# A written order in place of a greedy share: merging channel mixing with attention and token mixing

## The chip, the cores and the metric

The kernel runs on one core of a Trainium2 chip. The metric is device time in microseconds for one execution; the median of the runs is given, and one further execution was taken with the hardware profiler. Engines: TensorE (PE in the profile; its weight loads are PEld), VectorE (DVE), ScalarE (ACT), GpSimd (POOL) and SyncE (SP).

## The reference

Windowed attention with sink columns (window 128, 4 sinks) on q, k, v of shape (4, 8, 768, 64), and a mixer block on its result x of shape (4, 768, 512):

```
scores = q @ k.T / 8, kept where key < 4 or 0 <= row - key < 128
x = softmax(scores) @ v, heads side by side                       # (4, 768, 512)
h = relu(x.T @ w_tok1) @ w_tok2                                   # token mixing: 768 -> 256 -> 768
u = x + h.T
out = u + relu(u @ w_ch1) @ w_ch2                                 # channel mixing: 512 -> 1536 -> 512
```

## The kernel before

**Work.** A "pair" is two heads of one batch: 16 pairs, four a batch. Attention of a pair: q and k are transposed on TensorE; scores are made keys by rows, as 128-key blocks of which each serves two 128-row blocks; ScalarE takes the exponential out of PSUM into `pT`, VectorE masks it; the sums with `v_aug` (a column of ones appended) go back to PSUM (`ps_o`), and VectorE takes the reciprocal of the ones' column (`recip`) and multiplies into `x_sb`. Token mixing works on half a batch's columns (`g` = 0 for pairs 0 and 1 of the batch, 1 for pairs 2 and 3): `mix_h` (x times `w_tok1`, then relu into `h1T`), three `mix_u` (times `w_tok2`, plus x, into `u_sb`), and `turned_u`, which transposes `u_sb`; the copies out of PSUM make `uT`. Channel mixing of a batch is 24 units `v1` (four matmuls of 384 columns, relu into `v1T`) and then 24 units `out_part` (three matmuls of 512 columns; after every fourth VectorE adds u into `o_sb` and SP stores it). The last row block of batch 3 is split into three units by columns instead. A burst is a unit that works with parts of the array (64 rows) instead of all 128: transposes, scores, sink scores and sink values of neighbouring pairs are put together in bursts.

**Queues of units.** The kernel is written as an instruction stream by a small planner in the kernel file (class `Plan`). Every TensorE unit is an `Op` with its estimated ns, what it depends on, what PSUM banks it needs and which operations follow it on the other engines. There are two tags of PSUM: `sc`, two large banks for scores and transposes, and `mx`, four banks for everything else; a bank is free when its readers are done. `run` gets three sorts of units: `first` (attention of pairs 0 to 3 and batch 0's token mixing, several lists), `main` (channel mixing of batches 0 to 3: 48 + 48 + 48 + 47 units, of which the first 24 of a batch are `v1`) and `side` (attention of pairs 4 to 15 and token mixing of batches 1 to 3: 75 units). The planner keeps a clock for each engine and appends the next instruction; the other engines' operations come in the order in which the planner lets them begin, `urgent` deciding between those that can begin at the same time on the same engine. The chip then runs each engine's instructions in the order so written and waits for semaphores.

**How side and main were merged.** `target(m)` says how much of the side work (in estimated ns) should be placed when `m` of the main work is: batch b's channel mixing carries the side work for batch b + 1 in its first 60%. If side is behind, the next side unit is taken if it can begin within 40 ns of the next main unit, otherwise main first; if one of the two cannot begin, the other is taken.

**The side units by number** (index in `side`, as written by `attention_and_tokens`). "A" is a pair's first burst: transposes of the next pair, the first scores of this pair, and the sink values of the pair before, whose two `mx` banks it takes. "V" are the two value units of the pair before, one a head. "B" is the pair's second burst: its other scores, sink scores for two pairs and, at some pairs, a `turned_u`.

```
 0, 1        transposes of pair 4: q, k
 2, 3        pair 4: A, B
 4, 5 6, 7   pair 5: A, V of 4, B
 8, 9 10, 11 pair 6: A, V of 5, B;       12, 13-15  mix_h, mix_u of batch 1, g = 0
16, 17 18,19 pair 7: A, V of 6, B
20, 21 22    pair 8: A, V of 7;  23, 24-26  mix_h, mix_u of batch 1, g = 1;  27  B (turned_u)
28, 29 30,31 pair 9: A, V of 8, B
32, 33 34,35 pair 10: A, V of 9, B;      36, 37-39  mix_h, mix_u of batch 2, g = 0
40, 41 42,43 pair 11: A, V of 10, B
44, 45 46    pair 12: A, V of 11;  47, 48-50  mix_h, mix_u of batch 2, g = 1;  51  B (turned_u)
52, 53 54,55 pair 13: A, V of 12, B
56, 57 58,59 pair 14: A, V of 13, B;     60, 61-63  mix_h, mix_u of batch 3, g = 0
64, 65 66,67 pair 15: A, V of 14, B
68 69        values of pair 15;  70, 71-73  mix_h, mix_u of batch 3, g = 1;  74  turned_u
```

**Lines of the profile.** Matmuls are L113, with tiles `ps_mx<-uT,w_ch` for `v1` and `ps_mx<-w_ch,v1T` for `out_part`; transposes are L441 (`turned_u`), L471 and L453; copies are L120 (ScalarE) and L122 (VectorE, GpSimd), relu L126 and L128; exponentials L555 and L594, masks L563; `recip` L663 and `x_sb` L666; `u_sb` L767; `o_sb` L940; L489 is the memset that clears the score bank after a pair's transposes were copied out of it (`cleared`). `kTs` are the sink columns of k, copied out of the same bank as `kT`.

Of the kernel before, what the change touches and what calls it, by code (L numbers as in the profile page):

```python
# [16 lines left out]
def kernel(  # L17
# [14 lines left out]
    B, H, S, D = q.shape  # L32
# [10 lines left out]
    D1 = D + 1  # L43
    scale = 1.0 / float(D) ** 0.5

    NQ = 6
    MASKED_BY_PE = [(p, g) for p in range(NHP) for g in range(NT // 2) if (p, g) != (NHP - 1, 0)]

    singles = ctx.enter_context(tc.tile_pool(name="singles", bufs=1))
    qkv_pool = ctx.enter_context(tc.tile_pool(name="qkv", bufs=NQ))  # L50
    raw_pool = ctx.enter_context(tc.tile_pool(name="raw", bufs=4))
# [60 lines left out]
    def mm(*args, **kwargs):  # L112
        in_order(nc.tensor.matmul(*args, skip_group_check=True, **kwargs))  # L113
# [19 lines left out]
    done = {}  # L133
# [55 lines left out]
    for n in range(4):  # L189
        i, odd = n // 2, n % 2  # L190
# [27 lines left out]
    SWITCH = 95.0  # L218
# [23 lines left out]
    class Plan:  # L242
# [60 lines left out]
        def commit_pe(self, op, t):  # L303
# [7 lines left out]
            op.done = self.free["PE"] + PE_OUT + SEM  # L311
            self.pending.extend(op.then)

        def run(self, first, main, side, target):

            first, main, side = [list(u) for u in first], list(main), list(side)
            m = s = 0.0
            while any(first) or main or side or self.pending:
                o = self.other()
                tm = self.start_pe(main[0]) if main else None  # L320
                ts = self.start_pe(side[0]) if side else None
                early = [(t, u) for u in first if u for t in [self.start_pe(u[0])] if t is not None]
                if early:
                    soonest = min(t for t in [tm, ts, *(t for t, _ in early)] if t is not None)
                    stay = [(t, u) for t, u in early if self.half and u[0].half and t <= soonest + SWITCH]
                    t, u = next((e for e in stay + early if e[0] <= soonest + (SWITCH if e in stay else 40.0)), (None, None))
                    if u is not None and (o is None or o[0] > t):
                        self.commit_pe(u.pop(0), t)
                        continue
                pick = None  # L330
                if tm is not None and ts is not None:
                    behind = s < target(m)
                    if behind:
                        pick = "side" if ts <= tm + 40.0 else "main"
                    else:
                        pick = "main" if tm <= ts + 40.0 else "side"
                elif tm is not None:
                    pick = "main"
                elif ts is not None:
                    pick = "side"  # L340
                t = {"main": tm, "side": ts, None: None}[pick]
# [10 lines left out]
                assert pick, "no unit can begin"  # L352
                if pick == "main":
                    op = main.pop(0)
                    m += op.size
                else:
                    op = side.pop(0)
                    s += op.size
                self.commit_pe(op, t)

    def unit(ns, fn, deps=(), need=None, then=(), half=False):

# [281 lines left out]
    def sink_values(p):  # L644

        b, hp = pairs[p]
        vsk = v_sinks[p % NHP]

        def run():
            for i in range(2):  # L650
                tiles["ps_o", p, i] = bank("mx", NT, D1)
            for qt in range(2, NT):
                for i in range(2):
                    rows = ds(D * i, D)
                    mm(
                        tiles["ps_o", p, i][:, qt], tiles["pT_sink", p][rows, ts(qt - 2, P)], vsk[rows, i],
                        start=(qt == 2), stop=False,
                    )

        for i in range(2):  # L660
            def recip(e, i=i):
                r = tiles["recip", p, i] = pt_pool.tile([P, NT, 1], FP32, name="recip")
                in_order(nc.vector.reciprocal(r, tiles["ps_o", p, i][:, :, D:D1]))  # L663

            def norm(e, i=i):
                in_order(nc.vector.tensor_tensor(  # L666
                    out=x_sb[b][:, :, ds((2 * hp + i) * D, D)], in0=tiles["ps_o", p, i][:, :, 0:D],
                    in1=tiles["recip", p, i].to_broadcast([P, NT, D]), op=ALU.mult,
                ))

            done["r", p, i] = Op({"DVE": 180.0}, recip)
            done["x", p, i] = Op({"DVE": 550.0}, norm, [done["r", p, i]])
            done["r", p, i].urgent = done["x", p, i].urgent = 1
        return piece(
            120, run, [done["p", p, NT], done["vs", p]], {"mx": [[done[n, p, i] for n in "rx"] for i in range(2)]}, [],
        )
# [185 lines left out]
    def attention_and_tokens():  # L862
# [5 lines left out]
        for p in range(first, last + 1):  # L868
# [6 lines left out]
            if p > first:  # L875
                pieces.append(sink_values(p - 1))
# [135 lines left out]
    plan = Plan()  # L1012
# [53 lines left out]
    plan.pending.append(done["masks"])  # L1066

    first = first_attention()
    main, side, sizes = [], [], []
    parts = attention_and_tokens()  # L1070
    for b in range(B):
        units = parts[b] if b + 1 < B else []
        channels = mix_channels(b)
        sizes.append((sum(u.size for u in channels), sum(u.size for u in units)))
        main += channels
        side += units

    def target(m):
        total = 0.0
        for n, (msize, ssize) in enumerate(sizes):  # L1080
            f = m / msize / 0.6
            if f < 1.0 or n == B - 1:
                return total + max(0.0, min(1.0, f)) * ssize if m < msize else total + ssize
            if m < msize:
                return total + ssize
            total += ssize
            m -= msize
        return total

    plan.run(first, main, side, target)  # L1090


# [33 lines left out]
```

## Time and profile before

| | |
|---|---|
| median of 3 runs | 208.69 us (208.69 to 209.34) |
| the profiled execution | 208.97 us, of which the span is 207.2 us |
| granted TensorE clock | 1.00 of full speed |
| TensorE | 200.0 us busy, 97% of the span, 2377 matmuls |
| VectorE | 113.0 us, 55%, 253 instructions |
| ScalarE | 116.8 us, 56%, 213 instructions |
| GpSimd | 67.4 us, 33%, 86 instructions |
| loads by GpSimd's queue, share of 16 DMA engines | 72.3% |

The span runs from the first to the last profiled instruction; the execution's own time has some 1.8 us around it. The timeline rows read: start, length (us), engine, line, operation, tiles out<-in, shapes, count of merged instructions, and in brackets the engine's idle time just before and what ended it. Matmul rows overlap: one matmul's record is longer than the distance to the next.

### The profile page before, as it was taken

Reading aid. Unit: us, or ns where it says so; the run is one execution under the profiler, and the core shown is the slowest. Engines: PE = TensorE matmul, PEld = TensorE weight load, DVE = VectorE, ACT = ScalarE, POOL = GpSimd, SP = SyncE. Lnnn points to the kernel's source line nnn. Section 1 sums busy time; section 2 is a strip of 40 time slices with the busy share of each in tenths; the row PEclk is TensorE's granted clock in tenths of the full one; section 3 lists DMA queues with packets and bytes.
Section 4 is the critical chain, followed back from the end, with each engine's and each line's share of the span. In section 5 each row is a group of like instructions: output and inputs, shape, how many; then the busy total and the mean of one; then the engine's idle time right before and its main releaser. Section 6 shows DMA issues by size and latency. Waiting matters only on the chain.

```text
span 207.2 us, 5542 instructions
## 1 busy us (share of the span) xinstructions
PE 200.0 (97%) x2377; PEld 119.9 (58%) x2377; DVE 113.0 (55%) x253; ACT 116.8 (56%) x213; POOL 67.4 (33%) x86
## 2 busy tenths in 40 slices
PE   6899999999999999999999999999999999999994
PEld 2455885566665565656656555666756545665443
DVE  4686654747678657866586562856663621000222
ACT  4699767869717446979494141979671103774000
POOL 6399759795599982540000000000000000000000
PEclk9999999999999999999999999999999999999999
DMA  6999999999999999595000212100001122000223
GB/s 208 289 247 185 174 173 191 153 155 192 160 168 153 205 189 202 53 90 38 3 0 5 101 54 101 55 0 3 0 3 51 54 101 101 0 3 0 101 101 101
DMA packets 73223, 21.58 MB, mean 104 GB/s; under 512 B 63216, under 2 KB 70256, under 8 KB 73200
## 3 DMA queue, kind: packets, MB, share of 16 engines
q0 software_dynamic: 67232, 11.80, 72.3%
q1 hardware_dynamic: 5968, 9.45, 12.8%
q8 instruction: 18, 0.29, 0.6%
q14 instruction: 5, 0.04, 0.1%
HBM read 26.75 MB, written 6.29 MB: 159 GB/s over the span
## 4 chain that ended last, share of the span: by engine, by line
PE 88%; DVE 5%; ACT 3%; DMA 2%; issue 1%; SPq 0%
PE ps_mx L113 75%; PE ps_sc L113 7%; DMA k_f<-in_k_dram 2%; PE ps_sc L471 2%; DVE kT L122 2%; ACT qT L120 1%; PE ps_mx L441 1%; PE ps_mx L453 1%; DVE x_sb L666 1%; ACT pT L555 1%; ACT v1T L126 1%; PE ps_mx L116 1%; DVE uT L122 0%; DVE recip L663 0%; DVE u_sb L767 0%
## 5 line engine op out<-in xcount | busy, mean ns | idle before, releaser
L113 PE MATMUL ps_mx<-uT,w_ch 128*128 128x384 bf16 x384 | 67.9, 326 | 1.3 <-DVE x_sb L666 1.0
L113 PE MATMUL ps_mx<-w_ch,v1T 128*128 128x512 bf16 (+2 forms) x312 | 65.3, 363 | 0.0
L126 ACT ACTIVATE v1T<-ps_mx 128x384 bf16<-128x384 f32 x85 | 41.0, 494 | 26.8 <-PE ps_mx L113 17.6
L113 PEld LDWEIGHTS <-w_ch 128*128 128x128 bf16 x384 | 35.6, 98 | 25.7 <-DVE x_sb L666 2.5
L555 ACT ACTIVATE pT<-ps_sc 128x1024 bf16<-128x1024 f32 (+1 forms) x48 | 44.8, 957 | 9.3 <-PE ps_sc L113 8.7
L113 PEld LDWEIGHTS <-v1T 128*128 128x128 bf16 x312 | 29.1, 98 | 29.5 <-issue 0.2
L940 DVE TENSOR_TENSOR o_sb<-ps_mx,u_sb 128x512 f32<-128x512 f32 x23 | 15.9, 690 | 41.9 <-PE ps_mx L113 41.7
L98 POOL DMA_DIRECT2D q_bf<-in_q_dram x24 | 19.7, 824 | 4.5 <-DMA w_ch<-in_moe_w_ch_dram 2.2
L98 POOL DMA_DIRECT2D k_bf<-in_k_dram x24 | 19.6, 822 | 4.6 <-DMA w_ch<-in_moe_w_ch_dram 3.1
L113 PEld LDWEIGHTS <-w_tok 128*128 128x128 bf16 x192 | 18.3, 98 | 4.7 <-issue 0.7
L122 DVE COPY kT<-ps_sc 128x768 bf16<-128x768 bf16 x11 | 10.5, 958 | 16.7 <-ACT qT L120 16.7
L106 POOL DMA_DIRECT2D v_aug<-in_v_dram x16 | 16.5, 1030 | 9.5 <-ACT v1T L126 6.1
L563 DVE TENSOR_TENSOR pT<-pT,mask_main 128x1024 bf16<-128x1024 bf16 (+1 forms) x24 | 14.6, 620 | 4.4 <-ACT pT L555 4.4
L767 DVE TENSOR_TENSOR u_sb<-ps_mx,x_sb 128x512 bf16<-128x512 f32 x20 | 12.7, 685 | 5.0 <-PE ps_mx L113 5.0
L113 PE MATMUL ps_sc<-qT,kT 64*64 64x192 bf16 (+3 forms) x288 | 15.2, 252 | 0.2 <-DVE ps_sc L489 0.2
L113 PE MATMUL ps_mx<-v_aug,pT 128*128 128x65 bf16 x352 | 15.2, 194 | 0.0
L113 PEld LDWEIGHTS <-pT 128*128 128x128 bf16 x352 | 13.4, 98 | 1.9 <-issue 0.6
L120 ACT ACTIVATE qT<-ps_sc 128x768 bf16<-128x768 bf16 x11 | 8.9, 812 | 7.6 <-PE ps_sc L471 7.5
L113 PE MATMUL ps_mx<-h1T,w_tok 128*128 128x256 bf16 x96 | 12.5, 273 | 0.0
L113 PE MATMUL ps_mx<-x_sb,w_tok 128*128 128x256 bf16 x96 | 12.0, 273 | 0.0
L666 DVE TENSOR_TENSOR x_sb<-ps_mx,recip 128x384 bf16<-128x384 f32 x22 | 11.9, 542 | 0.0
L113 PEld LDWEIGHTS <-kT 64*64 64x64 bf16 (+1 forms) x288 | 7.1, 103 | 6.7 <-issue 5.0
(74 smaller groups left out, 156.0 us busy)
## 6 DMA issues: line engine op xcount, KB each, us to landing
out_dram<-o_sb SPq DMA_DIRECT2D x23, 256.0 KB, 2.0
v_aug<-in_v_dram POOLq DMA_DIRECT2D x16, 192.0 KB, 7.2
w_ch<-in_moe_w_ch_dram POOLq DMA_DIRECT2D x8, 384.0 KB, 9.0
q_bf<-in_q_dram POOLq DMA_DIRECT2D x24, 96.0 KB, 7.1
k_bf<-in_k_dram POOLq DMA_DIRECT2D x24, 96.0 KB, 6.0
q_f<-in_q_dram SPq DMA_DIRECT2D x4, 384.0 KB, 5.4
k_f<-in_k_dram SPq DMA_DIRECT2D x4, 384.0 KB, 5.9
w_tok<-in_moe_w_tok_dram POOLq DMA_DIRECT2D x2, 384.0 KB, 8.5
```

Of the source, the lines that this page charges most:

```text
L98: in_order(nc.gpsimd.dma_start(out=out[:, h], in_=rows[:, h]))
L106: in_order(nc.gpsimd.dma_start(out=v_aug.rearrange("p i t d -> p (i t) d")[:, :, 0:D], in_=v[b].rearrange("h s d -> (h s) d")[2 * hp * S:2 ...
L113: in_order(nc.tensor.matmul(*args, skip_group_check=True, **kwargs))
L120: in_order(nc.scalar.activation(out, in_, AF.Copy))
L122: in_order({"DVE": nc.vector, "POOL": nc.gpsimd}[e].tensor_copy(out=out, in_=in_))
L126: in_order(nc.scalar.activation(out, in_, AF.Relu))
L471: in_order(nc.tensor.transpose(ps[:, x, n, j], bfs[p, n][rows, j], ident[rows, rows]))
L555: in_order(nc.scalar.activation(part(tiles["pT", p][:, :, ds(2 * g, 2)]), of_keys(tiles["ps_s", p, g])[:, :, 0:width(g)], AF.Exp, scale=scale,
L563: in_order(nc.vector.tensor_tensor(out=pt, in0=pt, in1=m, op=ALU.mult))
L666: in_order(nc.vector.tensor_tensor(out=x_sb[b][:, :, ds((2 * hp + i) * D, D)], in0=tiles["ps_o", p, i][:, :, 0:D], in1=tiles["recip", p, i ...
L767: in_order(nc.vector.tensor_tensor(out=u_part(b, g, s0, n), in0=tiles["ps_u", b, g, s0], in1=x_sb[b][:, s0:s0 + n, c0:c0 + cn], op=ALU.add,))
L940: in_order(nc.vector.tensor_tensor(out=o_sb.rearrange("p (g c) -> p g c", g=2), in1=u_rows(b, st), in0=tiles["ps_out", b, st].rearrange("p ...
```

## The change

The shares (`target` and the sizes) are gone. `MERGED` lists the 75 side units in the order in which they are to be placed, each with the number of main units that must be placed before it ("23/41": side unit 23 when 41 main units are placed). `run` takes a side unit as soon as its number is reached, and otherwise main, and waits on its clock for that unit even if one of the other sort could begin. Units of `first` may still go before the picked one. Besides, the `recip` and `x_sb` operations of pairs 4 to 14 get the urgency 3 in place of 1 (the memset of the score bank has 2, the relu of `v1` has 1).

```diff
+    MERGED = (
+        "1/0 0/2 2/4 3/8 4/15 5/15 6/17 7/19 8/23 9/24 10/24 12/27 11/27 13/29 15/30 14/31 16/32 17/33 18/33 "
+        "19/36 20/39 21/39 22/39 23/41 25/42 24/42 26/42 27/44 28/49 29/50 30/51 31/52 32/57 33/58 34/58 "
+        "36/61 35/62 38/62 37/64 39/67 40/67 41/69 42/69 43/73 44/78 45/78 46/79 47/83 49/85 48/85 50/85 "
+        "51/90 52/98 53/100 55/102 54/107 56/107 57/108 58/108 59/113 60/115 62/118 63/121 61/121 64/124 "
+        "65/126 67/128 66/128 68/133 69/133 70/137 73/139 72/139 71/139 74/142"
+    )
...
-        def run(self, first, main, side, target):
...
+        def run(self, first, main, side):
+
+            first, main = [list(u) for u in first], list(main)
+            order = [[int(n) for n in unit.split("/")] for unit in MERGED.split()]
+            side, behind = [side[n] for n, _ in order], [n for _, n in order]
+            placed = 0
             while any(first) or main or side or self.pending:
                 o = self.other()
                 tm = self.start_pe(main[0]) if main else None
                 ts = self.start_pe(side[0]) if side else None
+                pick = "side" if side and (not main or behind[0] <= placed) else "main"
+                t = tm if pick == "main" else ts
                 early = [(t, u) for u in first if u for t in [self.start_pe(u[0])] if t is not None]
...
-                pick = None
-                if tm is not None and ts is not None:
-                    behind = s < target(m)
-                    if behind:
-                        pick = "side" if ts <= tm + 40.0 else "main"
-                    else:
-                        pick = "main" if tm <= ts + 40.0 else "side"
-                elif tm is not None:
-                    pick = "main"
-                elif ts is not None:
-                    pick = "side"
...
                 if pick == "main":
-                    op = main.pop(0)
-                    m += op.size
+                    placed += 1
                 else:
-                    op = side.pop(0)
-                    s += op.size
-                self.commit_pe(op, t)
+                    behind.pop(0)
+                self.commit_pe((main if pick == "main" else side).pop(0), t)
...
-            done["r", p, i].urgent = done["x", p, i].urgent = 1
+            done["r", p, i].urgent = done["x", p, i].urgent = 3
```

More of the change, by code (lines that the diff above doesn't have):

```diff
@@ L312, in commit_pe @@
             self.pending.extend(op.then)
-        def run(self, first, main, side, target):
-            first, main, side = [list(u) for u in first], list(main), list(side)
-            m = s = 0.0
+        def run(self, first, main, side):
[3 more added lines that the diff above has]
+            placed = 0
             while any(first) or main or side or self.pending:
@@ L321, in run @@
                 ts = self.start_pe(side[0]) if side else None
+                pick = "side" if side and (not main or behind[0] <= placed) else "main"
+                t = tm if pick == "main" else ts
                 early = [(t, u) for u in first if u for t in [self.start_pe(u[0])] if t is not None]
                 if early:
-                    soonest = min(t for t in [tm, ts, *(t for t, _ in early)] if t is not None)
+                    soonest = min([t for t, _ in early] + ([] if t is None else [t]))
                     stay = [(t, u) for t, u in early if self.half and u[0].half and t <= soonest + SWITCH]
-                    t, u = next((e for e in stay + early if e[0] <= soonest + (SWITCH if e in stay else 40.0)), (None, None))
-                    if u is not None and (o is None or o[0] > t):
-                        self.commit_pe(u.pop(0), t)
+                    te, u = next((e for e in stay + early if e[0] <= soonest + (SWITCH if e in stay else 40.0)), (None, None))
+                    if u is not None and (o is None or o[0] > te):
+                        self.commit_pe(u.pop(0), te)
                         continue
-                pick = None
-                if tm is not None and ts is not None:
-                    behind = s < target(m)
-                    if behind:
-                        pick = "side" if ts <= tm + 40.0 else "main"
-                    else:
-                        pick = "main" if tm <= ts + 40.0 else "side"
-                elif tm is not None:
-                    pick = "main"
-                elif ts is not None:
-                    pick = "side"
-                t = {"main": tm, "side": ts, None: None}[pick]
                 if o is not None and (t is None or o[0] <= t):
@@ L351, in run @@
                     continue
-                assert pick, "no unit can begin"
+                assert t is not None, "no unit can begin"
                 if pick == "main":
-                    op = main.pop(0)
-                    m += op.size
-                else:
-                    op = side.pop(0)
-                    s += op.size
-                self.commit_pe(op, t)
+                    placed += 1
+                else:
+                    behind.pop(0)
+                self.commit_pe((main if pick == "main" else side).pop(0), t)
     def unit(ns, fn, deps=(), need=None, then=(), half=False):
@@ L1068 @@
     first = first_attention()
-    main, side, sizes = [], [], []
+    main, side = [], []
     parts = attention_and_tokens()
     for b in range(B):
[L1072 to L1090, printed above, removed]
+        main += mix_channels(b)
+        side += parts[b] if b + 1 < B else []
+    plan.run(first, main, side)
 _INS = ['q', 'k', 'v', 'n_sink', 'window', 'moe_w_tok1', 'moe_w_tok2', 'moe_w_ch1', 'moe_w_ch2']
```

## The prediction

> **What bounds the kernel now.** I began with the page: the span, the busy time of each engine and the chain that ended last.
>
> ```profile
> span 207.2 us, 5542 instructions
> PE 200.0 (97%) x2377; PEld 119.9 (58%) x2377; DVE 113.0 (55%) x253; ACT 116.8 (56%) x213; POOL 67.4 (33%) x86
> ...
> PE 88%; DVE 5%; ACT 3%; DMA 2%; issue 1%; SPq 0%
> ...
> L113 PE MATMUL ps_mx<-uT,w_ch 128*128 128x384 bf16 x384 | 67.9, 326 | 1.3 <-DVE x_sb L666 1.0
> ```
>
> TensorE is busy for 200.0 of 207.2 us and is 88% of the chain. The change alters no matmul, so it can only win or lose time in which TensorE waits. The windows of the stretch in which the list acts, from the first channel matmul near 30 us to the last side unit near 165, and of the rest after it, show how much there is.
>
> ```profile
> 29.80:148.00 118.20, 116.50 (x1569) 71.04 (x1568) 77.52 (x163) 75.72 (x143) 45.70 (x54) 1.00 1.04 101
> 148.00:165.00 17.00, 17.00 (x229) 10.71 (x229) 9.65 (x21) 6.92 (x12) 0.00 (x0) 1.00 0.09 32
> 165.00:207.20 42.20, 39.26 (x230) 21.31 (x228) 7.42 (x13) 12.19 (x25) 0.00 (x0) 1.00 0.17 63
> ```
>
> The columns are length, then busy time (and count) of PE, PEld, DVE, ACT and POOL, then the clock. Idle are 118.20 - 116.50 = 1.70 us before 148 us, nothing from there to 165, and at the end only the tail after the last matmul, which the list does not touch. The granted clock is 1.00 throughout. Who ends the idle time stands in the view of waits (engine, line, releaser: total, times, longest):
>
> ```profile
> PE ps_mx L113 <- DVE x_sb L666: 1.0, 4, 0.2
> ...
> PE ps_mx L113 <- DVE uT L122: 0.4, 1, 0.4
> ...
> PE ps_sc L113 <- DVE ps_sc L489: 0.2, 1, 0.2
> ```
>
> These are idle times after the modelled end of the matmul before (326 ns after its start, while matmuls follow each other more closely), so each true loss is larger. The timelines of TensorE, VectorE and ScalarE around the first wait on `x_sb` show it.
>
> ```profile
> 44.05 0.84 PE L113 MATMUL ps_mx<-v_aug,pT 128*128 128x65 bf16 x22
> 44.73 1.46 PE L113 MATMUL ps_mx<-uT,w_ch 128*128 128x384 bf16 x8
> 46.43 0.82 PE L113 MATMUL ps_mx<-uT,w_ch 128*128 128x384 bf16 x4 [0.23 <-DVE x_sb L666]
> 47.18 0.49 PE L113 MATMUL ps_sc<-qT,kT 64*64 64x192 bf16 x16
> 47.60 3.42 PE L113 MATMUL ps_mx<-uT,w_ch 128*128 128x384 bf16 x20
> ```
> ```profile
> 44.72 0.96 DVE L122 COPY kT<-ps_sc 128x768 bf16<-128x768 bf16 x1 [2.11 <-ACT qT L120]
> 45.59 0.26 DVE L663 RECIPROCAL recip<-ps_mx 128x6 f32<-128x6 f32 x2
> 45.81 0.56 DVE L666 TENSOR_TENSOR x_sb<-ps_mx,recip 128x384 bf16<-128x384 f32 x1
> ```
> ```profile
> 43.88 0.81 ACT L120 ACTIVATE qT<-ps_sc 128x768 bf16<-128x768 bf16 x1
> 45.71 0.35 ACT L120 ACTIVATE kTs<-ps_sc 64x4 bf16<-64x4 bf16 x2 [1.02 <-DVE kT L122]
> 46.09 1.02 ACT L555 ACTIVATE pT<-ps_sc 128x1024 bf16<-128x1024 f32 x1
> 47.01 1.25 ACT L126 ACTIVATE v1T<-ps_mx 128x384 bf16<-128x384 f32 x3
> ```
>
> The row of 20 gives the pace: (3.42 - 0.33) / 19 = 0.163 us a matmul, 0.65 us for a first-product unit of four. Eight from 44.73 end their places at 44.73 + 8 x 0.163 = 46.03; the next began at 46.43: **0.40 us lost**. Both value units followed the burst at once, the burst had taken two of the four `mx` banks for them, two first-product units filled the other two, and the third found none. ScalarE could not empty one, because it copied `qT`, waited 1.02 us for `kT` and then did an exponential; VectorE copied `kT` only after `qT`, so its `x_sb` (45.81 + 0.56 = 46.37) was late as well. The four waits on `x_sb` are this picture (pairs 5, 10, 11 and 14), about 1.60 us in all.
>
> The wait on `uT` is at the boundary of batches 0 and 1:
>
> ```profile
> 80.31 0.50 PE L113 MATMUL ps_mx<-uT,w_ch 128*128 128x384 bf16 x2
> 81.17 0.48 PE L113 MATMUL ps_mx<-uT,w_ch 128*128 128x384 bf16 x2 [0.37 <-DVE uT L122]
> ```
> ```profile
> 80.10 1.02 DVE L122 COPY uT<-ps_mx 128x768 bf16<-128x768 bf16 x2 [0.16 <-PE ps_mx L441]
> ```
>
> 81.17 - 80.31 - 2 x 0.163 = **0.53 us**. Two bursts of scores wait for a bank: the one at 37.84 us by its idle row, the one at 54.48 us because its 16 matmuls take 0.72 us where the same 16 took 0.49.
>
> ```profile
> 37.84 0.49 PE L113 MATMUL ps_sc<-qT,kT 64*64 64x192 bf16 x16 [0.18 <-DVE ps_sc L489]
> ...
> 54.48 0.72 PE L113 MATMUL ps_sc<-qT,kT 64*64 64x192 bf16 x16
> ```
>
> That is 0.18 and 0.23. So about 1.60 + 0.53 + 0.41 = 2.54 us, 1.2% of the span, is all that an order of the merged stretch can win.
>
> **The change, part by part.** I number the units as the list does. Counting the channel matmuls in TensorE's timeline up to each side unit gives the old places, to be held against the new.
>
> *The boundary of batches 0 and 1.* Unit 27, whose transposes feed batch 1, went at 48 main units; it now goes at 44, four second-product units ahead of the first matmul that needs it. Those cover the two copies (1.02 us): 0.53 us gone. For batch 2 the places are 84 and 90 of 96, cover enough both times. For batch 3, unit 74 goes from 131 to 142 of 144. Two units, 1.3 us by the pace below, are to cover copies that can run on two engines; I take 0, and if one is queued behind an output addition, about 0.3.
>
> *The value units of pairs 5, 10, 11 and 14.* Old places of burst and both values: 15/15/15, 58/58/58, 67/67/67, 106/106/106. New: 15/15/17, 57/58/58, 67/69/69, 107/108/108. Old pair 9 (49/50/51) has such a spacing, shows no wait, and shows why:
>
> ```profile
> 82.39 0.82 PE L113 MATMUL ps_mx<-uT,w_ch 128*128 128x384 bf16 x4
> 83.05 0.50 PE L113 MATMUL ps_mx<-v_aug,pT 128*128 128x65 bf16 x11
> ```
> ```profile
> 83.25 0.49 ACT L126 ACTIVATE v1T<-ps_mx 128x384 bf16<-128x384 f32 x1 [0.22 <-PE ps_mx L113]
> ```
> ```profile
> 83.93 0.32 DVE L122 COPY kTs<-ps_sc 64x4 bf16<-64x4 bf16 x2
> ```
>
> A main unit between burst and values makes ScalarE empty its bank before the exponential. So pairs 10, 11 and 14 should lose about 0.08 instead of 0.40 each, a gain of 3 x 0.32 = 0.96. At pair 5 the first value unit still follows the burst: the third main unit needs a bank at 0.34 + 2 x 0.65 + 0.34 = 2.0 us after 44.05, and `x_sb` frees one at 46.37 + 0.05, 2.4 us after; with the switch to full tiles in it I put the loss at 0.25, a gain of 0.15. The bounds for the four are no gain and 1.60.
>
> *The scores of pair 6* (unit 11, at 54.48) now come behind a unit `mix_h` and one main unit more: 0.23 gone. Those of pair 4 keep their places 4 and 8: the 0.18 stays.
>
> *The second half of batch 1's token mixing*, units 20 to 27. Here the list asks more than the old order did. The old places were 40/40/40 for burst and values, 44 for `mix_h`, 46 for `mix_u`:
>
> ```profile
> 69.77 0.35 PE L471 MATMUL ps_sc<-ident,q_bf 64*128 64x64 bf16 x12
> ...
> 70.56 0.84 PE L113 MATMUL ps_mx<-v_aug,pT 128*128 128x65 bf16 x22
> 71.25 2.75 PE L113 MATMUL ps_mx<-w_ch,v1T 128*128 128x512 bf16 x12
> 73.83 1.47 PE L113 MATMUL ps_mx<-x_sb,w_tok 128*128 128x256 bf16 x12
> 75.14 1.46 PE L113 MATMUL ps_mx<-w_ch,v1T 128*128 128x512 bf16 x6
> ```
> ```profile
> 72.93 0.27 DVE L489 MEMSET ps_sc<- 64x256 f32 x1
> 73.12 0.53 DVE L666 TENSOR_TENSOR x_sb<-ps_mx,recip 128x384 bf16<-128x384 f32 x1
> ```
> ```profile
> 75.34 0.60 ACT L126 ACTIVATE h1T<-ps_mx 128x512 bf16<-128x512 f32 x1 [1.72 <-PE ps_mx L113]
> ```
>
> Twelve matmuls take 73.83 - 71.25 = 2.58 us, so a second-product unit of three takes 0.65. `mix_h` reads all of `x_sb`, whose last piece ended at 73.12 + 0.53 = 73.65, or 3.88 us after the burst's start. The new places are 39/39/39 and 41: two main units, not four, so `mix_h` comes at 71.25 + 1.30 - 69.77 = 2.78 us after the burst's start. The third edit, the normalisation's urgency of 3, lets the last `x_sb` pass the memset and saves 0.27, so it is there at about 3.61: with 0.05 for the semaphore a **new wait of 0.87 us**, and 1.15 without the saving. Behind it `mix_u` follows one main unit (0.65) after `mix_h` instead of two. `h1T` was done at 75.34 + 0.60 = 75.94, 0.80 after `mix_h` gave way at 75.14: **a wait of 0.20**. TensorE works in its written order, so all its later units queue behind these waits, and the other engines with them. Together 1.07; from 0, if the order on VectorE comes out otherwise, to 1.35.
>
> *The same question elsewhere.* The first halves for batches 1 and 2 (units 12 and 36) keep three main units behind values that now stand one main unit after their burst: 0.79 + 0.65 + 0.68 + 3 x 0.65 = 4.07 us after the burst's start against the 3.88 above, cover of 0.2 us. If VectorE also gets the two sink copies (0.32 above), it is gone. I take 0.05 each, 0 to 0.3. Units 47, 60 and 70 keep four or more. Unit 54, one value unit of pair 12, moves from 99 to 107 and holds one of four banks for 8 main units; three banks carry it if each is emptied within 1.3 us of its filling, and the ScalarE copy above began 0.2 us after its unit and took 0.49. I take 0, at most 0.4.
>
> *Queues.* Units 0 and 1 (the transposes of pair 4's q and k) only swap their places 0 and 2: 0, within 0.1. POOL's loads keep their order and SP's stores follow the outputs. No wait above is on a load.
>
> *Sum.* Gains 0.53 + 0.96 + 0.15 + 0.23 = 1.87; losses 1.07 + 0.10 = 1.17; net -0.70 us. The profiled execution took 208.97 us, 0.28 over the median of 208.69, so it would take 208.27 and the median is 207.99: **208.0 us**, 0.33% less.
>
> **A rule beside a row.** In every pair VectorE's `kT` begins as ScalarE's `qT` ends (43.88 + 0.81 = 44.69; 44.72), though the planner costs them side by side. The Trainium skill, "PSUM — Partial Sum Buffer", section "PSUM bank collisions raise a hardware error", says that ScalarE and VectorE may not touch one bank in the same quadrant together, not even for two reads, and that the compiler's scheduler orders them. The trace agrees with it here. Were it as the planner has it, every normalisation would end 0.84 us sooner and the wait of 0.87 would shrink to 0.03: a sum of -1.54 and a time of 207.2.
>
> **Rivals.** (1) *The normalisation comes early enough.* If VectorE finishes `x_sb` before `mix_h` wants it, as with `qT` and `kT` side by side or in another order on VectorE, the 0.87 goes and the net is -1.5: **207.2 us**. The idle 2.11 before `kT` speaks against it; for it speaks only that the last `x_sb` waits behind a memset that the urgency lets it pass. (2) *Sink copies ahead of the normalisation: slower.* With a main unit between burst and values, the planner gave `kTs` to VectorE (83.93, 0.32 us) instead of ScalarE. If it does so at all six normalisations that now have little cover, `mix_h` loses 0.32 more, units 12 and 36 about 0.2 each, and the 0.96 of pairs 10, 11 and 14 is lost again: -0.70 + 0.32 + 0.40 + 0.96 = +0.98, **209.7 us**. With k us more delay at all six the sum is -0.70 + 6k, so it turns at k = 0.12. For it speaks that row; against it that pair 9 showed no wait with it. (3) *The list changes nothing that counts*: many places are the old ones (4, 8, 15, 23, 29, 49 to 52), and gains and losses cancel: **208.7 us**.
>
> **How the numbers follow.** This kernel can be told from no change at about 0.3%, 0.63 us. I give the forecast 0.50, rival 1 0.18, rival 2 0.20, rival 3 0.12. The forecast lies close to that border: 0.30 of its 0.50 is beyond it, 0.20 within. Faster 0.30 + 0.18 = 0.48; same 0.20 + 0.12 = 0.32; slower 0.20. The range goes from a little below rival 1, where the pair 5 wait goes too, 207.0, to 209.5, short of rival 2's end. The forecast's own range is 207.5 to 208.6.
>
> **What would show it.** In the changed profile: no wait of TensorE on `uT` near 80 us; the waits on `x_sb` at first-product units down to one or two; a new wait on `x_sb`, 0.7 to 0.9 us, ahead of a `mix_h` near 72 us, and a short one on `h1T` behind it; the tail unchanged. I am wrong if that `mix_h` does not wait, if units 12 and 36 wait by tenths, if the four banks run short between 98 and 107 main units, or if batch 3's first channel matmuls wait for `uT`.

## The result, and the profile after

The median went from 209.02 us (7 runs, 208.69 to 209.51) to 208.02 us (7 runs, 207.5 to 208.35); the ratio is 0.995, with a 95% interval of 0.9933 to 0.9967. The forecast was 208.0, counted down by 0.70 from the 208.69 of the first three runs.

The page of the changed kernel, and its view of waits (engine, line, releaser: total us, times, longest):

```profile
span 205.7 us, 5537 instructions
...
PE 198.1 (96%) x2377; PEld 119.3 (58%) x2377; DVE 114.4 (56%) x261; ACT 116.5 (57%) x205; POOL 67.6 (33%) x86
...
PE 85%; DMA 6%; DVE 4%; POOL 1%; ACT 1%; issue 1%; SPq 0%; POOLq 0%
```
```profile
PE ps_mx L121 <- DVE x_sb L664: 0.7, 1, 0.7
...
PE ps_sc L121 <- DVE ps_sc L487: 0.2, 1, 0.2
```

The four short waits on `x_sb` and the one on `uT` are gone from this view; there is one long wait on `x_sb`, and pair 4's wait for the score bank's memset has stayed. The loads' larger part in the chain (DMA 6%, before 2%) lies ahead of 19 us, where the chain runs through the loads of `v_sink_f` and `w_tok`, and not in the merged stretch. The timelines of TensorE and VectorE at the one long wait:

```profile
67.91 0.35 PE L469 MATMUL ps_sc<-ident,q_bf 64*128 64x64 bf16 x12
...
69.39 1.46 PE L121 MATMUL ps_mx<-w_ch,v1T 128*128 128x512 bf16 x6
71.55 1.48 PE L121 MATMUL ps_mx<-x_sb,w_tok 128*128 128x256 bf16 x12 [0.70 <-DVE x_sb L664]
72.87 0.81 PE L121 MATMUL ps_mx<-w_ch,v1T 128*128 128x512 bf16 x3
73.72 1.36 PE L121 MATMUL ps_mx<-h1T,w_tok 128*128 128x256 bf16 x11
```
```profile
69.38 0.96 DVE L130 COPY kT<-ps_sc 128x768 bf16<-128x768 bf16 x1 [1.63 <-ACT qT L128]
70.25 0.26 DVE L661 RECIPROCAL recip<-ps_mx 128x6 f32<-128x6 f32 x2
70.47 1.02 DVE L664 TENSOR_TENSOR x_sb<-ps_mx,recip 128x384 bf16<-128x384 f32 x2
71.54 0.27 DVE L487 MEMSET ps_sc<- 64x256 f32 x1
```

Six matmuls from 69.39 take 6 x 0.215 = 1.29 us, so `mix_h` could have begun at 70.68; it began at 71.55, when the second `x_sb` was done (70.47 + 1.02 = 71.49): 0.87 us lost by these rows. Both `x_sb` now stand ahead of the memset. `mix_u` (73.72) lost 0.20 behind one second-product unit (72.87 + 0.65 = 73.52). At the boundary, unit 27's burst at 76.42 is followed by twelve matmuls without a break, and no wait on `uT` follows them:

```profile
76.42 0.49 PE L121 MATMUL ps_sc<-qT,kT 64*64 64x192 bf16 x16
76.72 0.60 PE L439 MATMUL ps_mx<-ident,u_sb 64*64 64x64 bf16 x48
77.26 0.40 PE L121 MATMUL ps_mx<-qT,kTs 64*32 64x512 bf16 x4
77.58 2.76 PE L121 MATMUL ps_mx<-w_ch,v1T 128*128 128x512 bf16 x12
```

**Where to measure from.** The two profiled spans differ by 1.5 us, more than the merged stretch explains. In TensorE's instruction order the two kernels are the same up to pair 4's transposes, yet these begin at different times:

```profile
30.84 0.35 PE L453 MATMUL ps_mx<-ident,q_bf 64*128 64x64 bf16 x12
```
```profile
30.06 0.35 PE L451 MATMUL ps_mx<-ident,k_bf 64*128 64x64 bf16 x12
```

The first row is of the old kernel, the second of the new. So 0.78 us of the difference lies ahead of anything that was changed. I compare the **stretch** from these transposes to the end of the span: 207.2 - 30.84 = 176.36 us before, 205.7 - 30.06 = 175.64 after, **0.72 us less**. The twelve kernels below, with the same program up to there, began it between 30.22 and 31.42 us. Each has one profile. What an edit leaves alone repeats closely in them: the wait at pair 4's scores, counted from start to start, is 0.23 to 0.25 us in all thirteen profiles whose kernel leaves its place alone.

### The profile page after: what moved, and what is told of

Read it like the earlier page. It is cut to its first block, busy times and chain, and to the rows that moved or that the text cites. A ratio compares the mean times of both kernels' runs of the same rounds, so it can differ in the third digit from the quotient of the medians.

```text
span 205.7 us, 5537 instructions
## 1 busy us (share of the span) xinstructions
PE 198.1 (96%) x2377; PEld 119.3 (58%) x2377; DVE 114.4 (56%) x261; ACT 116.5 (57%) x205; POOL 67.6 (33%) x86
## 4 chain that ended last, share of the span: by engine, by line
PE 85%; DMA 6%; DVE 4%; POOL 1%; ACT 1%; issue 1%; SPq 0%; POOLq 0%
PE ps_mx L121 77%; PE ps_sc L121 4%; DMA w_tok<-in_moe_w_tok_dram 4%; PE ps_sc L469 2%; DMA v_sink_f<-in_v_dram 2%; PE ps_mx L439 1%; POOL v_aug L114 1%; DVE kT L130 1%; ACT qT L128 1%; PE ps_mx L124 1%; DVE v1T L136 0%; ACT v1T L134 0%; DVE x_sb L664 0%; POOL v_sink L130 0%; SPq L200 0%
## 5 line engine op out<-in xcount | busy, mean ns | idle before, releaser
L121 PE MATMUL ps_mx<-w_ch,v1T 128*128 128x512 bf16 (+2 forms) x312 | 67.0, 363 | 0.0
L553 ACT ACTIVATE pT<-ps_sc 128x1024 bf16<-128x1024 f32 (+1 forms) x48 | 44.2, 952 | 13.8 <-PE ps_sc L121 13.4
L134 ACT ACTIVATE v1T<-ps_mx 128x384 bf16<-128x384 f32 x79 | 38.6, 490 | 20.7 <-PE ps_mx L121 20.0
L121 PEld LDWEIGHTS <-v1T 128*128 128x128 bf16 x312 | 28.4, 98 | 27.6 <-issue 0.7
L121 PEld LDWEIGHTS <-pT 128*128 128x128 bf16 x352 | 14.3, 97 | 3.2 <-issue 0.5
L121 PE MATMUL ps_sc<-qT,kT 64*64 64x192 bf16 (+3 forms) x288 | 14.5, 248 | 0.2 <-DVE ps_sc L487 0.2
L561 DVE TENSOR_TENSOR pT<-pT,mask_main 128x1024 bf16<-128x1024 bf16 (+1 forms) x24 | 14.0, 617 | 0.0
L121 PE MATMUL ps_mx<-h1T,w_tok 128*128 128x256 bf16 x96 | 13.4, 273 | 0.0
L134 ACT ACTIVATE h1T<-ps_mx 128x512 bf16<-128x512 f32 (+1 forms) x9 | 4.5, 504 | 13.9 <-PE ps_mx L121 13.8
L136 DVE TENSOR_SCALAR v1T<-ps_mx 128x384 bf16<-128x384 f32 x17 | 9.4, 555 | 4.6 <-PE ps_mx L121 4.1
```

The lines of the kernel that those rows point to most:

```text
L134: in_order(nc.scalar.activation(out, in_, AF.Relu))
L136: in_order(nc.vector.tensor_scalar_max(out=out, in0=in_, scalar1=0.0))
L553: in_order(nc.scalar.activation(part(tiles["pT", p][:, :, ds(2 * g, 2)]), of_keys(tiles["ps_s", p, g])[:, :, 0:width(g)], AF.Exp, scale=scale,
L561: in_order(nc.vector.tensor_tensor(out=pt, in0=pt, in1=m, op=ALU.mult))
```

## The experiments

My theory: the waits of the prediction, each with its own cause, which add up. Its rival: ScalarE and VectorE are loaded enough that a wait taken away comes back in the next place. A third: the list adds little, the urgency is the gain. Stretches in us, waits counted in TensorE's timeline from start to start as above; of `MERGED` the diffs show only the entries that change:

| kernel | stretch | against the new order |
|---|---|---|
| old order | 176.36 | +0.72 |
| new order | 175.64 | 0 |
| new list, urgency 1 | 177.72 | +2.08 |
| old places, urgency 3 | 176.50 | +0.86 |
| new list, unit 27 at 48 | 176.14 | +0.50 |
| new list, values right behind bursts | 176.58 | +0.94 |
| new list, tokens 2 later | 175.31 | -0.33 |
| new list, tokens spread | 174.97 | -0.67 |
| the same and three more places | 175.83 | +0.19 |
| new list, pair 9's kT on ScalarE | 175.78 | +0.14 |
| the same, sinks too, no addition between | 174.91 | -0.73 |
| the same, tokens a little later | 174.70 | -0.94 |
| old places, sinks on VectorE | 181.23 | +5.59 |
| the same, other bank | 181.29 | +5.65 |

### The third edit alone: urgency 1 with the new list

```diff
-            done["r", p, i].urgent = done["x", p, i].urgent = 3
+            done["r", p, i].urgent = done["x", p, i].urgent = 1
```

> The new list with the old urgency 1 of the normalisation. Lengths are of the stretch from the first transposes of pair 4 (near 30 us) to the end of the span: 176.36 us in the profile of the old order, 175.64 in that of the new. My theory, waits that add up: the last x_sb before batch 1's second mix_h falls behind the memset again, its wait grows from 0.87 to about 1.14, the other waits stay within 0.1, stretch 175.9. Rival, waits give way to each other (TensorE catches up on the busy neighbours later): stretch within 0.1 of 175.64.

Measured: 210.57 us, ratio to the old kernel 1.0071 (1.0027 to 1.0114). Both theories missed: +2.08. The wait at batch 1's second `mix_h` grew as expected, from 0.87 to 1.17, but other places got longer too, first unit 12, the other `mix_h` of batch 1. VectorE's and TensorE's timelines there:

```profile
53.96 0.27 DVE L487 MEMSET ps_sc<- 64x256 f32 x1
54.15 0.53 DVE L664 TENSOR_TENSOR x_sb<-ps_mx,recip 128x384 bf16<-128x384 f32 x1
54.60 0.17 DVE L661 RECIPROCAL recip<-ps_mx 128x6 f32<-128x6 f32 x1
54.70 0.64 DVE L561 TENSOR_TENSOR pT<-pT,mask_first 128x1024 bf16<-128x1024 bf16 x1
55.27 0.54 DVE L664 TENSOR_TENSOR x_sb<-ps_mx,recip 128x384 bf16<-128x384 f32 x1
```
```profile
55.87 1.38 PE L121 MATMUL ps_mx<-x_sb,w_tok 128*128 128x256 bf16 x11 [0.61 <-DVE x_sb L664]
```

Without the urgency a memset comes ahead of the first `x_sb` there, and the mask of an exponential (0.64 us) ahead of the second: unit 12 waits 0.78. At pairs 10 and 14 no mask comes between, but the memset and a relu do:

```profile
93.40 0.27 DVE L487 MEMSET ps_sc<- 64x256 f32 x1
93.59 0.53 DVE L664 TENSOR_TENSOR x_sb<-ps_mx,recip 128x384 bf16<-128x384 f32 x1
...
94.15 0.51 DVE L136 TENSOR_SCALAR v1T<-ps_mx 128x384 bf16<-128x384 f32 x1
94.58 0.54 DVE L664 TENSOR_TENSOR x_sb<-ps_mx,recip 128x384 bf16<-128x384 f32 x1
```

The bank waits of these two pairs are 0.28 each, and unit 36, which reads the `x_sb` of these rows, waits 0.34. Three more waits of about 0.1 make up the rest. The new list puts units so close behind their normalisations that each operation ahead of an `x_sb` shows.

### The urgency alone, with the old places

```diff
     MERGED = (the old places, counted in the old trace)
             done["r", p, i].urgent = done["x", p, i].urgent = 3
```

Written as a list with urgency 1, the old places give the old instruction order on every engine, so this kernel differs from the old one by the urgency only.

> The old places written as a list, with the new urgency 3. With urgency 1 the new list was 2.08 us longer (stretch 177.72). My theory: the urgency only matters where a unit is put right behind the normalisation it needs, which the old places hardly do; stretch within 0.4 of 176.36. Rival, that the urgency is the gain and the list adds nothing to it: stretch 175.9 or less.

Measured: 209.15 us, ratio 0.9998 (0.9976 to 1.0021); stretch 176.50, 0.14 more than the old. The urgency by itself wins nothing; together with the list it is a condition of the gain.

### The values of pairs 10, 11 and 14 put back

```diff
-32/57 33/58 34/58 ... 40/67 41/69 42/69 ... 56/107 57/108 58/108
+32/58 33/58 34/58 ... 40/67 41/67 42/67 ... 56/107 57/107 58/107
```

> The new list with the value units of pairs 10, 11 and 14 put right behind their bursts again (32/58, 41/67 and 42/67, 57/107 and 58/107). My theory: the third first-product unit behind each waits for a bank again, about 0.40 us each where the new list has 0 to 0.12, so 0.9 to 1.1 more, stretch 176.6 to 176.7, slower than the new order and about the old time. Rival, that the urgency or the other places removed those waits: stretch within 0.2 of 175.64.

Measured: 209.21 us, ratio 1.0005 (0.9991 to 1.0019); stretch +0.94. Its view of waits has the three back beside the long one:

```profile
PE ps_mx L121 <- DVE x_sb L664: 1.4, 4, 0.7
```

Each costs 0.40 from start to start, where the new list loses 0.11, 0 and 0.12.

### The tokens of batch 1 two or three units later

```diff
-23/41 25/42 24/42 26/42 27/44
+23/43 25/45 24/45 26/45 27/47
```

> The new list with units 23 to 27 two or three main units later: 23/43 25/45 24/45 26/45 27/47. My theory: the waits of 0.87 on x_sb and 0.20 on h1T both go, and one main unit plus the first two matmuls of the next still cover the copies of uT, so nothing comes for it: stretch 175.64 - 1.07 = 174.57, time about 0.5% under the new order and 1.0% under the old. Rival, waits give way to each other: under half of the 1.07 is won, the rest returns at the boundary of batches 0 and 1 as a wait on uT of 0.3 or more or at pair 9: stretch 175.1 or more.

Measured: 208.22 us, ratio 0.9961 (0.9937 to 0.9985); stretch -0.33. Both waits went, as I expected, and 0.74 came back on `uT`, as the rival had it. ScalarE's timeline says why:

```profile
78.74 1.73 ACT L553 ACTIVATE pT<-ps_sc 128x1024 bf16<-128x1024 f32 x2 [3.20 <-PE ps_sc L121]
80.35 0.82 ACT L128 ACTIVATE uT<-ps_mx 128x768 bf16<-128x768 bf16 x1
```
```profile
81.22 0.48 PE L121 MATMUL ps_mx<-uT,w_ch 128*128 128x384 bf16 x2 [0.57 <-ACT uT L128]
```

One of the two copies went to ScalarE, behind two exponentials, and ended at 81.17, 2.84 us after the burst (78.33), where VectorE with both had needed 1.02 us from 80.10. The place was not bad by itself: a copy's cover depends on which engine the planner gives it to.

### The tokens spread at both ends

```diff
-16/32 17/33 18/33 19/36 20/39 21/39 22/39 23/41 25/42 24/42 26/42 27/44
+16/31 17/32 18/32 19/35 20/38 21/38 22/38 23/41 25/43 24/43 26/43 27/45
```

> The new list with batch 1's second token half spread at both ends: 16/31 17/32 18/32 19/35 20/38 21/38 22/38 23/41 25/43 24/43 26/43 27/45. In the last experiment the wait moved: the 1.07 went, and 0.74 came at the boundary because one copy of uT went to ScalarE behind two exponentials and ended 2.84 us after the burst's start. My theory, waits that add up once each cover is long enough for its real chain: three main units after the values leave about 0.2 of the 0.87, two after mix_h none of the 0.20, three after the burst cover the copies; stretch 175.64 - 0.87 = 174.8. Rival, what is taken away there comes back in another wait: stretch 175.3 or more, as 175.31 was.

Measured: 207.84 us, ratio 0.9937 (0.9914 to 0.9959); stretch -0.67 where I expected -0.87. The wait at `mix_h` was 0.22, those on `h1T` and `uT` zero; 0.19 came new at pair 7's second scores. An output addition had come ahead of the normalisation on VectorE, and the scores waited for the score bank's memset behind both (65.22 + 0.27 = 65.49):

```profile
63.33 0.68 DVE L938 TENSOR_TENSOR o_sb<-ps_mx,u_sb 128x512 f32<-128x512 f32 x1
...
65.22 0.27 DVE L487 MEMSET ps_sc<- 64x256 f32 x1
```

### Three more places

```diff
-2/4 3/8 4/15 5/15 6/17 ... 53/100 55/102 54/107 56/107 57/108 58/108
+2/4 3/9 4/15 5/16 6/17 ... 53/99 54/100 55/102 56/107 57/108 58/109
```

> The list of the run before, and besides 3/9 for pair 4's second scores, 4/15 5/16 6/17 for pair 5, and 53/99 54/100 and 57/108 58/109 for the values of pairs 12 and 13, each with one main unit ahead as pair 9 has it. My theory: the waits of 0.24, 0.23, 0.16 and 0.12 there go as well, stretch 174.8 - 0.75 = 174.0, time some 0.8% under the new order. Rival: they come back nearby, stretch 174.6 or more.

Measured: 207.81 us, ratio 0.9955 (0.9928 to 0.9983); stretch 0.86 longer than the run before instead of 0.8 shorter. Of the four waits one went (0.24, pair 4's scores). Three grew: at pair 5 from 0.23 to 0.38, at the values of pair 12 from 0.16 to 0.23, at those of pair 13 (pair 14's burst) from 0.12 to 0.29. And TensorE waited 0.61 for a slice of `w_ch2`:

```profile
54.94 0.81 PE L121 MATMUL ps_mx<-w_ch,v1T 128*128 128x512 bf16 x3 [0.45 <-DMA w_ch<-in_moe_w_ch_dram]
```

Reading a good spacing off one pair and copying it to others failed here: without the wait for the load the stretch is still 0.25 longer. The wait for the load need not be the list's. The profiled execution took 208.62 us, 0.81 more than the median of the ten, and by the medians this kernel and the run before are alike (207.81 and 207.84).

### The boundary put back

```diff
-23/41 25/42 24/42 26/42 27/44 28/49
+23/41 25/42 24/42 26/42 27/48 28/49
```

> The new list with unit 27 at 48 again, the boundary of batches 0 and 1, all else as new. My theory: the wait of 0.53 on uT is back if VectorE makes both copies, up to 1.4 if one goes to ScalarE behind the exponentials as two runs before; stretch 176.2 to 177.0. Rival, that the old wait came from the burst's late mix_u and not from its place: stretch within 0.2 of 175.64.

(The copy behind the exponentials is that of the tokens placed later, above.)

Measured: 208.63 us, ratio 0.9981 (0.9962 to 1.0); stretch +0.50, and TensorE waits 0.53 for `uT` again, both copies being VectorE's. The gain of 0.53 at the boundary is shown.

### What sets the long wait: kT on ScalarE

```diff
-Op(dict(cost), lambda e, n=n, part=part: evict(e, n, part), free[n])
+Op({"ACT": 900.0} if n and p == 9 else dict(cost), lambda e, n=n, part=part: evict(e, n, part), free[n])
```

> The new list with one copy moved: kT of pair 9 (the burst ahead of batch 1's second mix_h) is made by ScalarE, idle there, behind qT, in place of VectorE. My theory, the chain qT, kT, normalisation sets the wait: with kT off VectorE both x_sb are ready about 0.8 us sooner, the wait of 0.87 falls under 0.15, the one of 0.20 on h1T stays within 0.1, stretch about 174.9. Rival, mix_h waits for something behind the normalisation (a bank, or the output addition on VectorE): the wait stays over 0.5 and the stretch over 175.3.

Measured: 208.18 us, ratio 0.9962 (0.9946 to 0.9978); the wait was 1.04, not under 0.15: a miss. The first `x_sb` did end 0.5 us sooner after the burst, but the planner then put an output addition of 0.65 us ahead of the second, as the rival had it. So the chain was tried again with that addition kept out, `kT` still on ScalarE and the sink columns with it:

```diff
+            {"ACT": 440.0} if p == 9 else {"ACT": 440.0, "DVE": 400.0}, sink_columns, ...
...
-            done["r", p, i] = Op({"DVE": 180.0}, recip)
+            done["r", p, i] = Op({"DVE": 180.0}, recip, lag=0.0 if p == 7 else None)
```

> The new list; of pair 9 both kT and the sink columns go to ScalarE, and the recip of pair 7 is planned without a semaphore's delay, so that VectorE's order is recip, x_sb, recip, x_sb with no output addition between (in the run with kT alone on ScalarE the first x_sb ended 0.5 us sooner, but an output addition of 0.65 us came ahead of the second). My theory, the chain qT, kT, normalisation sets mix_h's wait: VectorE can begin with recip as the first value unit ends, needs 0.19 + 0.56 + 0.15 + 0.53, the second x_sb is there 2.8 us after the burst's start instead of 3.6, and the wait falls from 0.86 to 0.1 or less; stretch 174.9. Rival: mix_h waits for a bank or for ScalarE; the wait stays over 0.5 and the stretch over 175.3.

Measured: 207.56 us, ratio 0.9931 (0.9905 to 0.9957); stretch 174.91, the wait 0.11. VectorE's timeline, with the burst at 68.85:

```profile
70.19 0.20 DVE L661 RECIPROCAL recip<-ps_mx 128x6 f32<-128x6 f32 x1 [1.50 <-PE ps_mx L121]
70.42 0.56 DVE L664 TENSOR_TENSOR x_sb<-ps_mx,recip 128x384 bf16<-128x384 f32 x1
70.90 0.18 DVE L661 RECIPROCAL recip<-ps_mx 128x6 f32<-128x6 f32 x1
71.11 0.56 DVE L664 TENSOR_TENSOR x_sb<-ps_mx,recip 128x384 bf16<-128x384 f32 x1
```

The last `x_sb` is done 71.67 - 68.85 = 2.82 us after the burst's start, where it was 3.58. From the burst to the last `x_sb`, VectorE's work differs from the new kernel's by the missing `kT` alone, apart from the order of the two `recip` and the two `x_sb` among themselves. The copy of `kT`, which follows that of `qT`, ahead of the normalisation is what set the long wait: shown.

### A version that beats both

```diff
 (the kernel above)
-23/41 25/42 24/42 26/42 27/44
+23/41 25/43 24/43 26/43 27/45
```

> The kernel of the run above with 23/41 25/43 24/43 26/43 27/45 in place of 23/41 25/42 24/42 26/42 27/44: two main units after mix_h, three at the boundary. My theory: mix_h's wait 0.1 or less, no wait on h1T, none on uT; stretch 175.64 - 0.77 - 0.20 = 174.7, time some 0.45% under the new order, 0.95% under the old. Rival, waits give way to each other: stretch 175.2 or more.

Measured: **207.31 us**, ratio 0.9929 (0.9905 to 0.9953), stretch 174.70: the wait at `mix_h` 0.11, none on `h1T` or `uT`. By the stretch it is 0.94 us under the new order; by the ratios alone the two intervals overlap.

### What the x_sb waits of the old order were

```diff
 (the old places, urgency 1)
-            {"ACT": 440.0, "DVE": 400.0}, sink_columns, ...
+            {"DVE": 400.0} if p > NHP else {"ACT": 440.0, "DVE": 400.0}, sink_columns, ...
```

> The old places with the old urgency; only the sink columns of pairs 5 to 15 are always VectorE's, which puts them behind the normalisation, so that ScalarE does not wait 1.02 us for kT between qT and the exponential. My theory, the four waits of 0.40 are for a bank, and ScalarE's order is half of their cause: its relu frees a bank about as early as x_sb does, and each falls to 0.1 to 0.3; stretch 176.36 - 0.4 to - 1.2. Rival, x_sb alone sets them: they stay at 0.35 to 0.40 and the stretch within 0.2 of 176.36.

Measured: 213.81 us, ratio 1.0242 (1.0209 to 1.0275). The four waits stayed at 0.40, as the rival had it, and the stretch grew by 4.87, which neither had. ScalarE's and TensorE's timelines show that a bank emptied sooner by ScalarE does not end these waits:

```profile
45.30 0.49 ACT L134 ACTIVATE v1T<-ps_mx 128x384 bf16<-128x384 f32 x1
```
```profile
46.15 0.82 PE L121 MATMUL ps_mx<-uT,w_ch 128*128 128x384 bf16 x4 [0.23 <-DVE x_sb L664]
46.90 0.36 PE L121 MATMUL ps_sc<-qT,kT 64*64 64x192 bf16 x8
47.89 0.33 PE L121 MATMUL ps_sc<-qT,kT 64*64 64x192 bf16 x8 [0.63 <-DVE ps_sc L487]
```

ScalarE had emptied a first-product unit's bank at 45.79, and TensorE waited on for `x_sb` until 46.15. The planner names each unit's bank when it writes the instructions; this unit had been given the value units'. The 4.87 us come from elsewhere: VectorE now does the normalisation, the sink copies, a mask and only then the memset, and the scores waited for it 0.56 to 1.20 us longer at six places. The new theory was tried by the planner's choice alone:

```diff
-            return sorted(free)
+            return sorted(free, key=lambda f: f[0] + 700.0 * any(getattr(r, "norm", 0) for r in self.held[tag][f[1]]))
...
+            done["x", p, i].norm = 1
```

> The run before (old places, sink columns on VectorE behind the normalisation) left the four waits of 0.40 on x_sb as they were, though ScalarE had emptied the first-product unit's bank 0.3 us earlier. New theory: a bank is picked when the instructions are written, by the planner's clock, and the third first-product unit was given the value units' bank; TensorE waits for that bank whatever else is free. Here the planner's choice alone is changed: among free mx banks it prefers, by 700 ns of its clock, one that no normalisation held. The theory: at pairs 5, 10, 11 and 14 the wait on x_sb is gone (under 0.1), and TensorE waits as much longer for the score bank's memset behind it (0.79 to about 1.2), the stretch stays within 0.3 of 181.23. Rival, the normalisation is needed for something else than a bank: the waits on x_sb stay at 0.4.

Measured in a single run: 213.76 us, stretch 181.29. The wait on `x_sb` at the four pairs is under 0.1, and the scores behind wait that much longer:

```profile
44.60 2.20 PE L121 MATMUL ps_mx<-uT,w_ch 128*128 128x384 bf16 x12
46.73 0.36 PE L121 MATMUL ps_sc<-qT,kT 64*64 64x192 bf16 x8
48.04 0.33 PE L121 MATMUL ps_sc<-qT,kT 64*64 64x192 bf16 x8 [0.94 <-DVE ps_sc L487]
```

Twelve matmuls pass now with no wait of note between. The waits were for a bank chosen beforehand; and here waits did give way to each other, since the memset's time did not move. In the old order itself no bank was empty sooner: ScalarE's next relu began there at 47.01, behind the `x_sb` that ended at 46.37.

## Why the prediction was right

By its steps, with the forecast first and the new profile second:

- *Boundary of batches 0 and 1*: 0.53 to go; gone, and 0.53 back when unit 27 is put back.
- *Pairs 10, 11, 14*: 0.08 each to stay; 0.11, 0 and 0.12. Three of 0.40 are back with the old spacing.
- *Pair 5*: 0.25 to stay; 0.23. *Pair 6's scores*: 0.23 to go; gone. *Pair 4's scores*: 0.18 to stay; 0.24, which is what they lost in the old trace too, from start to start (0.25).
- *Second `mix_h` of batch 1*: 0.87 to come; 0.87. *`mix_u` behind it*: 0.20; 0.20.
- *Units 12 and 36*: 0.05 each; none. *Unit 54 and its bank*: 0, at most 0.4; 0.16 at the second main unit behind pair 12's first value unit, 101 main units in. The banks did run short there, by little; the prediction names that as a sign of being wrong. *Batch 3's first channel matmuls*: 0; none.
- *Sum*: -0.70 us; -0.72 in the stretch. The waits counted in the two traces come to 2.6 and 1.9 us, so they account for it within 0.1. The timed median fell by 1.0; the interval of the ratio, 0.69 to 1.40 us of 209.02, just holds the 0.72. What the median shows beyond it is not explained by the list; it is within what the start varies. That 208.02 stands so near to 208.0 is luck in part: three runs put the old kernel at 208.69 and seven at 209.02, 0.33 higher, and the fall was 0.30 larger than forecast.

Two steps were wrong without harm to the sum. The **urgency** was sized at 0.27 us, at one `mix_h`; with the new list it is worth 2.08, 0.30 of it there. The prices of the other places go by rows of the old order, in which a memset or a relu stands ahead of an `x_sb`, but no mask; the prediction does not reckon that the new places need the urgency as well. The change gave it to them, so this part came right by luck. And the **cause of the `x_sb` waits** was incomplete: no bank was empty, as the prediction says, but TensorE waits for the bank that the program names, and one emptied sooner by ScalarE would have changed nothing. Nor does the spacing help by another bank: behind the values of pairs 10, 11 and 14 the new kernel's planner again gives the third first-product unit a value unit's bank. It helps because the values come later behind the burst, and so `x_sb` sooner behind the values. Pair 10 in TensorE's and VectorE's new timelines:

```profile
89.69 0.83 PE L121 MATMUL ps_mx<-v_aug,pT 128*128 128x65 bf16 x22
90.36 2.23 PE L121 MATMUL ps_mx<-uT,w_ch 128*128 128x384 bf16 x12
```
```profile
91.16 1.02 DVE L664 TENSOR_TENSOR x_sb<-ps_mx,recip 128x384 bf16<-128x384 f32 x2
```

The first `x_sb`, 0.56 us long as before, ends at 91.72, 2.03 us behind the start of the values, where the old order had 46.37 - 44.05 = 2.32. That is the 0.29 by which the wait fell, from 0.40 to 0.11.

Rival 1 is out: the normalisation did not come early enough; with `kT` off VectorE it does, and the wait is 0.11. The row of `kT` behind `qT` stands in the new trace as well: VectorE began at 69.38 after 1.63 us of idling for `qT`. It stands so for the eleven pairs from 5 on, whose two transposes share a score bank, and not "in every pair". The Trainium skill's rule on one bank and two readers ("PSUM — Partial Sum Buffer", "PSUM bank collisions raise a hardware error") agrees with these rows; that it is their cause was not tried. Rival 2 is out as a whole: VectorE took the sink copies of pairs 10 and 14 without a wait of more than 0.12. Rival 3 is out by the interval.

## What to carry to other kernels

Where one engine is busy 97% of its span, price a new order by its waits alone: count each unit's cover in units of the busy engine and hold it against the time from the producer's start to the last copy, read from the trace. A wait that a removed one uncovers lay here mostly with an in-order neighbour (an exponential, an addition, a memset, a mask, put ahead of the copy that is waited for), so look at that engine's order, and at which bank the program names, before moving a unit. Compare single profiles from the first instruction that differs.

## What was not expected of the hardware

The start of one and the same program differs by over a microsecond between executions. TensorE's timelines of the old kernel and of the new in the first microseconds, where both run the same instructions:

```profile
6.18 1.89 PE L113 MATMUL ps_sc<-mask_add,ident 128*128 128x512 bf16 x4
8.00 1.03 PE L113 MATMUL ps_sc<-qT,kT 64*128 64x256 bf16 x8
```
```profile
6.02 1.04 PE L121 MATMUL ps_sc<-mask_add,ident 128*128 128x512 bf16 x4
6.99 0.61 PE L121 MATMUL ps_sc<-qT,kT 64*128 64x256 bf16 x8
```

The same four matmuls took 1.89 us in one and 1.04 in the other, while the profile's clock row shows full speed in both. The Trainium skill, "TensorE: Matmul & The Clock Gate", section "What's actually happening", has the array at half rate until about 3.4 us of activity are counted in a window that runs freely, so that the number of slow matmuls at the start changes from run to run. The two lengths of these four matmuls agree with two such rates; that the window is the cause here was not tried.

The slow matmuls do not settle where the merged stretch begins, though. Of the 14 profiles, seven have these four at 1.04 us and begin it between 30.06 and 30.98 us; six have them at 1.89 and begin it between 30.71 and 31.42; one has 1.39 and 30.57. The two groups overlap: the new list with urgency 1 has the fast four and begins later (30.98) than the old kernel with the slow four (30.84). TensorE's other waits of the first 30 us differ as well, for example 1.5 us for `q_bf` in that profile and 0.9 us for the load of `v_aug` in that of the three more places. What sets the start is open.
